# Work ahead of the first group in another order, the last group split 12 to 4: a convolution with a fused MLP

## The chip, the cores and the metric

The kernel runs on one core of a Trainium2 chip, in 32-bit floats throughout. The metric is the device time of one execution in microseconds (us). The core has a matrix engine (PE in the profile; its weight loads, which overlap, are listed as PEld), a vector engine (DVE), an activation engine (ACT), a general engine (POOL) and a queue engine (SP) that here only issues DMAs. Each engine takes its instructions in the order in which the program gives them; they meet through semaphores.

## The reference, cut to what matters

```python
# x: 8 x 4224 x 192, weight: 8 heads x 7 taps, g_ln: 192, w_ch1: 192 x 768, w_ch2: 768 x 192
w = softmax(weight, axis=-1)                       # 7 taps for each of 8 heads of 24 channels
y[b, s, h, :] = sum_k w[h, k] * x_pad[b, s + k, h, :]   # causal, 6 zero rows in front
mu, var = mean(y, -1), mean((y - mu)**2, -1)
xn  = (y - mu) / sqrt(var + 1e-6) * g_ln
out = y + max(xn @ w_ch1, 0) @ w_ch2
```

The inputs w_ch1 and w_ch2 are 64-bit floats in memory. The kernel reads them as pairs of 32-bit words and builds 32-bit floats from these itself.

## The kernel before, in words

**Groups.** The 33,792 tokens are worked on in 18 groups. A group has 128 partitions with n tokens each: group 0 has n = 6, group 1 n = 8, group 2 n = 10, and all from group 3 on n = 16. For each group the kernel convolves (`first_tap` and `second_tap` on ACT, `conv` on DVE, one instruction per tap and head), transposes 32 x 32 blocks on DVE (`transpose`), multiplies by w1 on PE (`up` for groups 0 to 2, `up_mixed` from group 3), evicts with a ReLU, multiplies by w2 (`down` for groups 0 and 1, `down_fast` from 2), transposes back and adds the result, scaled by the reciprocal root of the variance, to y. The scaling is put last because the ReLU lets a positive factor through. `up_mixed` and `down_fast` need seven products where a plain 2 x 2 block product needs eight; they form sums of quarters of their operands first (`sums_of_y`, `w1sums`, `w2sums`, `half_sum`).

**Order.** All orders are written out by hand (`manual_schedule`). PE runs `up(g)`, `down(g)`, `up(g+1)` and so on; the other engines prepare group g + 1 and finish group g - 1 meanwhile.

**Ahead of the first group** (lines 178 to 372 and 970 to 999). SP issues the load of w1's words in four pieces, then x of group 0 in three (`load_x`, L168 and L175). The taps go through a softmax. `split_words` (L232 to L245) takes mantissa and exponent out of each of three pieces of w1 (128 x 384 words each): DVE, ACT, DVE, DVE, ACT. `join_words` puts them together: L250 adds the low word (DVE), L253 sets the sign (DVE), L261 multiplies and applies g_ln, whose two columns `gs` ACT copies out of PSUM (L980). A memset of one word of `raw2` (L985) behind the first joined piece holds back the load of w2's words (L986) until then, and with it the eight loads of group 1's x that SP issues next (L142).

The convolution of group 0 is divided: DVE and ACT take heads 0 to 4, PE heads 5 to 7 (`PE_HEADS`). For a head on PE, ACT writes seven diagonal matrices, a tap each (`tap_matrices`, L319), PE multiplies x by them (`conv_on_pe`, L326), ACT copies the sum into y (L330). `centre_w1` subtracts the mean over the 192 channels from w1, so that mu drops out of the product: PE forms the means (L335, L339), ACT copies them (L342), and then PE makes four copies of each 32-row block of w1, in three steps of four (pieces s = 0, 2, 1), with the copy product L354 and the subtraction L359; ACT evicts them into `w1` (L364). The first step fills columns 0 to 383 of blocks 0 to 3, the second blocks 4 and 5, the third columns 384 to 767 of blocks 0 to 3. `up(0)` goes through six chunks f of 128 columns, so that chunks 0 to 2 read nothing of the third step. `keep_warm` (L369) issues idle matmuls of a constant tile `less`, which nobody reads.

The scratch tile `room` is cut into parts by `carve`, in the order of the calls. Group 0's hidden tile later lies on its first 4608 columns.

**During up(0).** ACT evicts each chunk (L525). The mantissa of w2 runs on DVE and ACT (`split_words`), its exponent is scaled by ACT behind chunk 0 (`scale_power`), and `join_words` makes w2 on DVE, all of it before the convolution of group 1. `first_tap(1)` takes heads 0 to 3 behind chunk 0 and 4 to 7 behind chunk 1. PSUM has eight banks: `take_bank` takes the next one, `take_set` the next aligned four, and each chunk of `up` takes four.

**The last group.** Its 16 tokens a partition are divided. `fast[NG - 1]` of them (11) go through `down_fast` with width 176; the hidden rows of the others are put aside by ACT (`keep`, L752), and `down_rows` (L959) multiplies six pieces of 128 for each such token. DVE adds each token to y (L942); one store takes all fast tokens (L949), and one each of the others.

Of the kernel before, what the change touches and what calls it, by code (L numbers as in the profile page):

```python
# [16 lines left out]
def kernel(  # L17
# [56 lines left out]


    fast = {g: groups[g][2] if g >= 3 else 0 for g in range(NG)}
    fast[NG - 1] = J - 5
    fast[2] = groups[2][2]
    NFAST = max(fast.values())
    T = C // 2  # L80
# [39 lines left out]
    def take_bank():  # L120
        i = turn[0] % 8
        turn[0] = i + 1
        return all_banks[:, i]
# [63 lines left out]
    def carve(n, dtype):  # L187
        part = room[:, taken[0] : taken[0] + n].bitcast(dtype)
        taken[0] += n
        return part  # L190

    less = carve(P, F32)
    nc.gpsimd.memset(less, -1.0 / C)

    raw1 = carve(6 * FH, U32).rearrange("p (s f w) -> p s f w", f=FH, w=2)
    raw2 = opool.tile([P, J * D], F32, tag="ot", name="raw2")[:, 0 : 2 * NF * D].bitcast(U32)
    raw2 = raw2.rearrange("p (n w) -> p n w", w=2)
    w1_words = moe_w_ch1.bitcast(U32)
# [45 lines left out]
    def scale_power(power):  # L244
        nc.scalar.activation(power, power, AF.Relu, scale=float(1 << 23), bias=low)  # L245

    def join_words(dst, raw, mant, power, g=None):
        lo, hi = raw[:, :, 0], raw[:, :, 1]
        mant, power = mant.bitcast(F32), power.bitcast(U32)
        nc.vector.scalar_tensor_tensor(  # L250
            out=mant, in0=lo, scalar=2.0**-52, in1=mant, op0=ALU.mult, op1=ALU.add
        )
        nc.vector.scalar_tensor_tensor(  # L253
            out=power, in0=hi, scalar=0x80000000, in1=power,
            op0=ALU.bitwise_and, op1=ALU.bitwise_or,
        )
        power = power.bitcast(F32)
        if g is None:
            nc.vector.tensor_tensor(dst, mant, power, op=ALU.mult)
            return  # L260
        nc.vector.scalar_tensor_tensor(  # L261
            out=dst, in0=mant, scalar=g, in1=power, op0=ALU.mult, op1=ALU.mult
        )
# [13 lines left out]
    nc.vector.tensor_tensor(  # L277
        taps, taps, wsum.unsqueeze(2).to_broadcast([P, H, K]), op=ALU.mult
    )
    words_1 = [(raw1[:, s], carve(FH, I32), carve(FH, I32)) for s in range(3)]  # L280

    w1 = consts.tile([P, NC, F], F32, name="w1")
    w2flat = consts.tile([P, NF * D], F32, name="w2")
    w2 = w2flat.rearrange("p (c d) -> p c d", d=D)
# [29 lines left out]
    def tap_matrices(h, ks=range(K)):  # L317
        for k in ks:
            nc.scalar.mul(diag[:, h - PE_HEADS[0], k, :], unit, taps[:, h, k : k + 1])  # L319
# [12 lines left out]
    def centre_w1():  # L332
        pm = [take_bank()[:, 0:FH] for r in range(2)]
        for r in range(2):
            nc.tensor.matmul(pm[r], share[0], w1f[:, r, :], start=True, stop=False)  # L335
            if r == 0:
                conv_on_pe(PE_HEADS[2])
        for r in range(2):
            nc.tensor.matmul(pm[r], share[1 + r], w1f[:, 2, :], start=False, stop=True)  # L339
        tap_matrices(PE_HEADS[1])  # L340
        for r in range(2):
            nc.scalar.copy(mean[:, FH * r : FH * r + FH], pm[r])  # L342
        conv_on_pe(PE_HEADS[0])
        conv_on_pe(PE_HEADS[1])

        for s, parts in (
            (0, [(q, 0) for q in range(NQ)]),
            (2, [(NQ, 0), (NQ + 1, 0), (NQ, 1), (NQ + 1, 1)]),
            (1, [(q, 1) for q in range(NQ)]),
        ):  # L350
            pw = [take_bank() for q in range(NQ)]
            for q in range(NQ):
                rows = slice(C * q, C * q + C)
                nc.tensor.matmul(  # L354
                    pw[q][:, 0:FH], copy[rows], w1f[rows, s, :], start=True, stop=False
                )
            for q, (c, r) in enumerate(parts):
                rows = slice(C * q, C * q + C)
                nc.tensor.matmul(  # L359
                    pw[q][:, 0:FH], less[rows], mean[rows, FH * r : FH * r + FH],  # L360
                    start=False, stop=True,
                )
            for q, (c, r) in enumerate(parts):
                nc.scalar.copy(w1[:, c, FH * r : FH * r + FH], pw[q][:, 0:FH])  # L364
    def keep_warm(times):

        idle = take_bank()
        for _ in range(times):
            nc.tensor.matmul(idle[:, 0:P], less, less, start=True, stop=True)  # L369

# [187 lines left out]
    def up(g):  # L558


        n = groups[g][2]
        hidden_tile(g)
        for f in range(NF):
            banks = take_set()
            rows_of_tiles(banks, yt[g][:, 0:n], w1[:, :, f * P : f * P + P])
            evict_up(g, f, banks[:, :, 0 : n * C])
            if g == 0 and f == 0:
                scale_power(words_2[2])
                join_words(w2flat, *words_2)
            if g == 0 and f < 2:  # L570
                first_tap(1, heads=(H // 2 * f, H // 2 * (f + 1)))
            between(g, f)

    def quarters_of_w1(f0=0, f1=FC):
# [392 lines left out]
            )  # L967


    keep_warm(17)  # L970
    g_cols = take_bank()
    for r in range(2):
        nc.tensor.matmul(
            g_cols[:, r : r + 1], g_row[:, P * r : P * r + P], ones[:, 0:1], start=True, stop=True
        )
    for s in range(3):
        split_words(*words_1[s])
        if s == 0:
            tap_matrices(PE_HEADS[2], range(3))
    nc.scalar.copy(gs, g_cols[:, 0:2])  # L980
    tap_matrices(PE_HEADS[2], range(3, K))
    for s in range(3):
        join_words(w1f[:, s], *words_1[s], ga if s < 2 else gb)
        if s == 0:
            nc.vector.memset(raw2[0:1, 0:1, :], 0)  # L985
    nc.sync.dma_start(  # L986
# [1 line left out]
        in_=w2_words.rearrange("(c p) d -> p c d", p=P),  # L988
    )
    load_x(1)  # L990
    first_tap(0, heads=(0, PE_HEADS[0]))
    tap_matrices(PE_HEADS[0])
    conv(0, heads=(0, PE_HEADS[0]))
    centre_w1()
    transpose(0)
# [16 lines left out]
    for g in range(NG):  # L1012
# [8 lines left out]
            work = []  # L1021
        if g == 0:
            early = CH * C // GRP
            conv(1, heads=(0, early))
            transpose(1, 0, CH)
            conv(1, heads=(early, H))
            first_tap(2)
            second_tap(2)
            let_in(w1sums[:, 1])
            transpose(1, CH, NC)  # L1030
            load_x(3)
            store_y(1)
            moments(0)
            moments(1)
            sums_of_quarters(w1sums[:, 1], w12, w22)
            sums_of_quarters(w1sums[:, 0], w11, w1sums[:, 1])
            next(root(0, True))
        elif g == 1:
            conv(2, 2)
            transpose(2)  # L1040
            first_tap(3)
            add_second_tap(3, 6)
            sums_of_quarters(w2sums[:, 2], b12, b22)
            sums_of_quarters(w2sums[:, 0], b12, b11)
            sums_of_quarters(w2sums[:, 1], b22, w2sums[:, 0])
            sums_of_quarters(w2sums[:, 3], b21, w2sums[:, 1])
            load_x(4, nc.gpsimd, pad=False)
            store_y(2, nc.gpsimd)
        elif g == 2:
            conv(3, 2, 5, heads=(0, 6))  # L1050
            lower_sum(2)
            conv(3, 5, K, heads=(0, 6))
            let_in(w1sums[:, 2])
            sums_of_quarters(w1sums[:, 2], w21, w1sums[:, 0])
# [54 lines left out]
```

## Time and profile before

| | |
|---|---|
| three timed runs | 956.90, 957.18, 958.33 us; median 957.18 |
| the profiled execution | 957.49 us, of which span 955.5 us |
| PE busy | 946.9 us (99%) |
| DVE / ACT / POOL busy | 891.3 / 699.0 / 337.1 us |
| granted PE clock | 1.00 |
| up(0) and down(0) on PE | 24.1 to 49.06 us |
| from the last group's first `down_rows` to the end of the span | 942.4 to 955.5 us |

A share of busy time is an average over the span. The span begins a little before the first instruction, and about 2 us of the execution lie outside it. In a timeline a line gives the start, the time from there to the end of the group, the engine, the line of the code, the operation, the tiles (written <- read), shapes and count; the bracket has the idle time before it and what ended it. A 32-bit matmul leaves two records in the trace, so that its counts are twice those of the program.

### The profile page before, as it was taken

How to read it: one execution, taken by the hardware profiler on the slowest of the kernel's cores; microseconds unless marked ns; L12 is line 12 of the kernel's file. 1: busy time of each engine (PE TensorE's matmuls, PEld its weight loads, DVE VectorE, ACT ScalarE, POOL GpSimd, SP SyncE). 2: the span in 40 equal slices, each digit the busy share in tenths (PEclk: the TensorE clock that was granted, in tenths of full speed). 3: DMA queues.
4: the chain of work that ended last, by engine and by line, in shares of the span. 5: the costliest groups of instructions: out<-in, count | busy, mean ns of one | idle time of the engine just before them, and what ended most of it. 6: DMA issues, size and time to landing. Idle time of an engine off the chain costs nothing.

```text
span 955.5 us, 38716 instructions
## 1 busy us (share of the span) xinstructions
PE 946.9 (99%) x17262; PEld 726.1 (76%) x17262; DVE 891.3 (93%) x1500; ACT 699.0 (73%) x1174; POOL 337.1 (35%) x472
## 2 busy tenths in 40 slices
PE   8999999999999999999999999999999999999998
PEld 6886896876869687786968778695867869586787
DVE  7999999999999999999999999999999999999757
ACT  6754678596877959687795968779695877967462
POOL 1157522623145141534227141452316332261320
PEclk9999999999999999999999999999999999999999
DMA  8359689689697988979697896969889696778251
GB/s 209 105 154 212 110 221 281 120 182 235 135 262 140 246 160 185 221 133 276 129 251 150 194 220 128 277 128 253 158 195 209 126 275 133 175 135 141 40 98 68
DMA packets 39691, 168.87 MB, mean 177 GB/s; under 512 B 4453, under 2 KB 8294, under 8 KB 33511
## 3 DMA queue, kind: packets, MB, share of 16 engines
q0 software_dynamic: 32576, 106.25, 60.0%
q1 hardware_dynamic: 6944, 60.16, 17.2%
q8 instruction: 135, 2.21, 0.9%
q14 instruction: 30, 0.25, 0.1%
q10 hardware_dynamic: 6, 0.00, 0.0%
HBM read 38.93 MB, written 50.33 MB: 93 GB/s over the span
## 4 chain that ended last, share of the span: by engine, by line
PE 95%; DMA 2%; ACT 1%; POOL 1%; issue 0%; SPq 0%; DVE 0%; ACTq 0%; POOLq 0%
PE ps L535 46%; PE ps L838 44%; PE ps L785 3%; PE ps L959 1%; DMA xg<-in_x_dram 1%; DMA room<-room 1%; PE ps L326 1%; ACT room L645 1%; ACT w L364 0%; POOL room L612 0%; POOL d L462 0%; POOL r L485 0%; POOL d L481 0%; ACT y L382 0%; ACT spare L245 0%
## 5 line engine op out<-in xcount | busy, mean ns | idle before, releaser
L419 DVE SCALAR_TENSOR_TENSOR y<-xg,taps,y 128x384 f32<-128x384 f32 (+3 forms) x720 | 362.6, 579 | 1.0 <-issue 0.8
L838 PE MATMUL ps<-room,w2sums 128*32 128x256 f32 (+2 forms) x4608 | 246.2, 370 | 0.4 <-issue 0.4
L535 PE MATMUL ps<-yt,w 32*128 32x256 f32 (+2 forms) x4104 | 235.5, 379 | 0.4 <-ACT room L525 0.4
L645 ACT COPY room<-ps 128x1024 f32<-128x1024 f32 (+1 forms) x135 | 175.0, 1296 | 78.4 <-PE ps L535 78.0
L535 PEld LDWEIGHTS ps<-yt,w 32*128 32x128 f32 x4104 | 204.6, 185 | 25.6 <-issue 9.0
L838 PEld LDWEIGHTS ps<-room,w2sums 128*32 128x32 f32 x4608 | 148.3, 110 | 92.4 <-ACT room L658 5.3
L838 PE MATMUL ps<-room,w 128*32 128x256 f32 (+2 forms) x3456 | 188.2, 370 | 0.1
L805 DVE TENSOR_TENSOR room<-room 128x1024 f32<-128x1024 f32 (+2 forms) x147 | 160.6, 1166 | 20.7 <-PE ps L838 20.7
L838 PEld LDWEIGHTS ps<-room,w 128*32 128x32 f32 x3456 | 111.3, 110 | 69.0 <-DVE room L651 5.0
L535 PE MATMUL ps<-ysums,w1sums 32*128 32x256 f32 x2160 | 125.6, 379 | 0.0
L535 PEld LDWEIGHTS ps<-ysums,w1sums 32*128 32x128 f32 x2160 | 109.4, 185 | 11.1 <-ACT room L645 3.6
L938 POOL DMA_DIRECT2D out_dram<-ot x69 | 59.3, 990 | 161.3 <-ACT ot L927 104.7
L411 POOL DMA_DIRECT2D y<-tb x59 | 52.5, 1386 | 152.7 <-ACT room L844 110.2
L844 ACT COPY cs<-ps 128x256 f32<-128x256 f32 (+2 forms) x192 | 69.9, 366 | 44.3 <-PE ps L838 44.3
L927 ACT ACTIVATE ot<-ot,r 128x192 f32<-128x192 f32 x232 | 93.8, 463 | 0.0
L658 ACT ACTIVATE room<-room 128x1024 f32<-128x1024 f32 (+1 forms) x89 | 92.8, 1072 | 1.4 <-DMA room<-parts_cs 1.2
L382 ACT ACTIVATE y<-xg,taps 128x384 f32<-128x384 f32 (+3 forms) x141 | 73.1, 611 | 1.5 <-DMA xg<-in_x_dram 1.5
L450 DVE BATCH_NORM_STATS2 st<-y 128x6 f32<-128x192 f32 x264 | 70.2, 345 | 0.0
L844 ACT COPY room<-ps 128x256 f32<-128x256 f32 (+2 forms) x96 | 35.2, 367 | 45.6 <-PE ps L838 43.6
L400 ACT ACTIVATE tb<-xg,taps 128x384 f32<-128x384 f32 (+1 forms) x120 | 65.9, 624 | 0.0
L535 PE MATMUL ps<-yt,w1sums 32*128 32x256 f32 x1080 | 65.3, 380 | 0.1
L535 PE MATMUL ps<-ysums,w 32*128 32x256 f32 x1080 | 64.5, 376 | 0.0
(113 smaller groups left out, 907.3 us busy)
## 6 DMA issues: line engine op xcount, KB each, us to landing
xg<-in_x_dram SPq DMA_DIRECT2D x14, 2112.0 KB, 16.5
room<-room POOLq DMA_DIRECT2D x45, 512.0 KB, 5.2
out_dram<-ot POOLq DMA_DIRECT2D x59, 384.0 KB, 9.4
y<-tb POOLq DMA_DIRECT2D x58, 384.0 KB, 8.8
out_dram<-y SPq DMA_DIRECT2D x13, 1536.0 KB, 9.1
room<-parts_cs POOLq DMA_DIRECT2D x28, 512.0 KB, 6.8
room<-parts_tb POOLq DMA_DIRECT2D x14, 1024.0 KB, 7.6
xg<-in_x_dram POOLq DMA_DIRECT2D x1, 2112.0 KB, 14.5
```

The costliest lines, as they stand in the source:

```text
L382: nc.scalar.mul(y[g][:, 0:n, cs], xg[g][:, 0:n, cs], taps[:, h, 0:1])
L400: nc.scalar.mul(tb[g][:, 0:n, cs], xg[g][:, 1 : 1 + n, cs], taps[:, h, 1:2])
L419: nc.vector.scalar_tensor_tensor(out=y[g][:, 0:n, cs], in0=t[:, k : k + n, cs], scalar=taps[:, h, k : k + 1], in1=y[g][:, 0:n, cs], op0=AL ...
L450: nc.vector.bn_stats(out=sums[g][:, j, :], in_=y[g][:, j, :])
L535: nc.tensor.matmul(banks[:, q, i * w : i * w + w], right[rows, c, P * i : P * i + P], left[rows, :, c, :], start=(first and c == 0 and i = ...
L645: nc.scalar.activation(dst, src, AF.Relu) if relu else nc.scalar.copy(dst, src)
L658: nc.scalar.activation(c, c, AF.Relu)
L805: nc.vector.tensor_tensor(a[:, *dst, f], a[:, *left, f], a[:, *right, f], op=op)
L838: nc.tensor.matmul(dst[C * q : C * q + C, 0:w], right[:, f, C * c : C * c + C], left[:, f, q], start=(first and f == PAIR), stop=(f == PAI ...
L844: nc.scalar.copy(to[:, c], dst[:, 0:w].rearrange("p (j t) -> p j t", t=t))
L927: nc.scalar.mul(ots[g][:, j, :], ots[g][:, j, :], rstd[g][:, j : j + 1])
L938: nc.gpsimd.dma_start(out=rows[:, d0:d1], in_=src[:, d0:d1], accum_op=ALU.add)
```

## The change

The last group's fast tokens go from 11 to 12, and the rest from five to four. The parts of `room` are cut in another order: w1's words and their work tiles first, which together are the 4608 columns of group 0's hidden tile, then `less` and the rest. `join_words` becomes three functions. On DVE the low word and sign of the first piece of w1 come ahead of the split of the third piece. On PE nine idle matmuls stand ahead of the columns of g_ln and fourteen behind them, and two more in `centre_w1` in place of the convolution of head 7, which moves behind the second mean product. On ACT `gs` is copied before the third split, four of head 5's matrices are made ahead of `first_tap(0)`, and the matrices of head 6 are made in two parts. The convolutions of heads 5 and 6 on PE are each followed by one step of copies of w1. The third step of copies moves behind chunk 1 of `up(0)`, with `scale_power` of w2 behind it. `first_tap(1)` takes heads 0 to 3 behind chunk 0, none behind chunk 1, two behind chunk 2 and two behind chunk 3. On DVE the convolution of group 1's first four heads is cut at tap 5, and the sign and product of w2 stand in the cut.

```diff
--- before.py
+++ after.py
@@ -74,7 +74,7 @@
 
 
     fast = {g: groups[g][2] if g >= 3 else 0 for g in range(NG)}
-    fast[NG - 1] = J - 5
+    fast[NG - 1] = J - 4
     fast[2] = groups[2][2]
     NFAST = max(fast.values())
     T = C // 2
@@ -189,10 +189,11 @@
         taken[0] += n
         return part
 
+    raw1 = carve(6 * FH, U32).rearrange("p (s f w) -> p s f w", f=FH, w=2)
+    words_1 = [(raw1[:, s], carve(FH, I32), carve(FH, I32)) for s in range(3)]
     less = carve(P, F32)
     nc.gpsimd.memset(less, -1.0 / C)
 
-    raw1 = carve(6 * FH, U32).rearrange("p (s f w) -> p s f w", f=FH, w=2)
     raw2 = opool.tile([P, J * D], F32, tag="ot", name="raw2")[:, 0 : 2 * NF * D].bitcast(U32)
     raw2 = raw2.rearrange("p (n w) -> p n w", w=2)
     w1_words = moe_w_ch1.bitcast(U32)
@@ -244,17 +245,21 @@
     def scale_power(power):
         nc.scalar.activation(power, power, AF.Relu, scale=float(1 << 23), bias=low)
 
-    def join_words(dst, raw, mant, power, g=None):
-        lo, hi = raw[:, :, 0], raw[:, :, 1]
-        mant, power = mant.bitcast(F32), power.bitcast(U32)
+    def join_low(raw, mant, power):
+        mant = mant.bitcast(F32)
         nc.vector.scalar_tensor_tensor(
-            out=mant, in0=lo, scalar=2.0**-52, in1=mant, op0=ALU.mult, op1=ALU.add
+            out=mant, in0=raw[:, :, 0], scalar=2.0**-52, in1=mant, op0=ALU.mult, op1=ALU.add
         )
+
+    def join_sign(raw, mant, power):
+        hi, power = raw[:, :, 1], power.bitcast(U32)
         nc.vector.scalar_tensor_tensor(
             out=power, in0=hi, scalar=0x80000000, in1=power,
             op0=ALU.bitwise_and, op1=ALU.bitwise_or,
         )
-        power = power.bitcast(F32)
+
+    def join_product(dst, raw, mant, power, g=None):
+        mant, power = mant.bitcast(F32), power.bitcast(F32)
         if g is None:
             nc.vector.tensor_tensor(dst, mant, power, op=ALU.mult)
             return
@@ -277,11 +282,6 @@
     nc.vector.tensor_tensor(
         taps, taps, wsum.unsqueeze(2).to_broadcast([P, H, K]), op=ALU.mult
     )
-    words_1 = [(raw1[:, s], carve(FH, I32), carve(FH, I32)) for s in range(3)]
-
-
-
-
     w1 = consts.tile([P, NC, F], F32, name="w1")
     w2flat = consts.tile([P, NF * D], F32, name="w2")
     w2 = w2flat.rearrange("p (c d) -> p c d", d=D)
@@ -334,37 +334,35 @@
         for r in range(2):
             nc.tensor.matmul(pm[r], share[0], w1f[:, r, :], start=True, stop=False)
             if r == 0:
-                conv_on_pe(PE_HEADS[2])
+                keep_warm(2)
+        conv_on_pe(PE_HEADS[2])
         for r in range(2):
             nc.tensor.matmul(pm[r], share[1 + r], w1f[:, 2, :], start=False, stop=True)
-        tap_matrices(PE_HEADS[1])
+        tap_matrices(PE_HEADS[1], range(3))
         for r in range(2):
             nc.scalar.copy(mean[:, FH * r : FH * r + FH], pm[r])
+        tap_matrices(PE_HEADS[1], range(3, K))
         conv_on_pe(PE_HEADS[0])
+        copies_of_w1(0, [(q, 0) for q in range(NQ)])
         conv_on_pe(PE_HEADS[1])
-
-        for s, parts in (
-            (0, [(q, 0) for q in range(NQ)]),
-            (2, [(NQ, 0), (NQ + 1, 0), (NQ, 1), (NQ + 1, 1)]),
-            (1, [(q, 1) for q in range(NQ)]),
-        ):
-            pw = [take_bank() for q in range(NQ)]
-            for q in range(NQ):
-                rows = slice(C * q, C * q + C)
-                nc.tensor.matmul(
-                    pw[q][:, 0:FH], copy[rows], w1f[rows, s, :], start=True, stop=False
-                )
-            for q, (c, r) in enumerate(parts):
-                rows = slice(C * q, C * q + C)
-                nc.tensor.matmul(
-                    pw[q][:, 0:FH], less[rows], mean[rows, FH * r : FH * r + FH],
-                    start=False, stop=True,
-                )
-            for q, (c, r) in enumerate(parts):
-                nc.scalar.copy(w1[:, c, FH * r : FH * r + FH], pw[q][:, 0:FH])
+        copies_of_w1(2, [(NQ, 0), (NQ + 1, 0), (NQ, 1), (NQ + 1, 1)])
+
+    def copies_of_w1(s, parts):
+        pw = [take_bank() for q in range(NQ)]
+        for q in range(NQ):
+            rows = slice(C * q, C * q + C)
+            nc.tensor.matmul(pw[q][:, 0:FH], copy[rows], w1f[rows, s, :], start=True, stop=False)
+        for q, (c, r) in enumerate(parts):
+            rows = slice(C * q, C * q + C)
+            nc.tensor.matmul(
+                pw[q][:, 0:FH], less[rows], mean[rows, FH * r : FH * r + FH],
+                start=False, stop=True,
+            )
+        for q, (c, r) in enumerate(parts):
+            nc.scalar.copy(w1[:, c, FH * r : FH * r + FH], pw[q][:, 0:FH])
+
     def keep_warm(times):
 
-        idle = take_bank()
         for _ in range(times):
             nc.tensor.matmul(idle[:, 0:P], less, less, start=True, stop=True)
 
@@ -565,10 +563,12 @@
             rows_of_tiles(banks, yt[g][:, 0:n], w1[:, :, f * P : f * P + P])
             evict_up(g, f, banks[:, :, 0 : n * C])
             if g == 0 and f == 0:
+                first_tap(1, heads=(0, H // 2))
+            elif g == 0 and f == 1:
+                copies_of_w1(1, [(q, 1) for q in range(NQ)])
                 scale_power(words_2[2])
-                join_words(w2flat, *words_2)
-            if g == 0 and f < 2:
-                first_tap(1, heads=(H // 2 * f, H // 2 * (f + 1)))
+            elif g == 0 and f < 4:
+                first_tap(1, heads=(2 * f, 2 * f + 2))
             between(g, f)
 
     def quarters_of_w1(f0=0, f1=FC):
@@ -967,20 +967,27 @@
             )
 
 
-    keep_warm(17)
+    idle = take_bank()
+    keep_warm(9)
     g_cols = take_bank()
     for r in range(2):
         nc.tensor.matmul(
             g_cols[:, r : r + 1], g_row[:, P * r : P * r + P], ones[:, 0:1], start=True, stop=True
         )
-    for s in range(3):
-        split_words(*words_1[s])
-        if s == 0:
-            tap_matrices(PE_HEADS[2], range(3))
+    keep_warm(14)
+    split_words(*words_1[0])
+    tap_matrices(PE_HEADS[2], range(3))
+    split_words(*words_1[1])
     nc.scalar.copy(gs, g_cols[:, 0:2])
+    join_low(*words_1[0])
+    join_sign(*words_1[0])
+    split_words(*words_1[2])
     tap_matrices(PE_HEADS[2], range(3, K))
     for s in range(3):
-        join_words(w1f[:, s], *words_1[s], ga if s < 2 else gb)
+        if s:
+            join_low(*words_1[s])
+            join_sign(*words_1[s])
+        join_product(w1f[:, s], *words_1[s], ga if s < 2 else gb)
         if s == 0:
             nc.vector.memset(raw2[0:1, 0:1, :], 0)
     nc.sync.dma_start(
@@ -988,8 +995,9 @@
         in_=w2_words.rearrange("(c p) d -> p c d", p=P),
     )
     load_x(1)
+    tap_matrices(PE_HEADS[0], range(4))
     first_tap(0, heads=(0, PE_HEADS[0]))
-    tap_matrices(PE_HEADS[0])
+    tap_matrices(PE_HEADS[0], range(4, K))
     conv(0, heads=(0, PE_HEADS[0]))
     centre_w1()
     transpose(0)
@@ -1021,7 +1029,11 @@
             work = []
         if g == 0:
             early = CH * C // GRP
-            conv(1, heads=(0, early))
+            join_low(*words_2)
+            conv(1, 1, 5, heads=(0, early))
+            join_sign(*words_2)
+            join_product(w2flat, *words_2)
+            conv(1, 5, K, heads=(0, early))
             transpose(1, 0, CH)
             conv(1, heads=(early, H))
             first_tap(2)
```

## The prediction

> **What bounds the kernel now.** I read the page first, then the chain of waits, then the timelines of the two ends. The page's first line says how much there is to win at all:
>
> ```profile
> PE 946.9 (99%) x17262; PEld 726.1 (76%) x17262; DVE 891.3 (93%) x1500; ACT 699.0 (73%) x1174; POOL 337.1 (35%) x472
> ```
>
> PE idles 8.6 us of the 955.5 us span. The chain says where. These are pieces of it in the first 55 us (start, duration, what):
>
> ```profile
> 3.51 8.84 DMA xg<-in_x_dram
> 12.44 1.95 PE ps L326 x14
> ...
> 24.61 1.35 ACT w L364 x3
> ...
> 28.85 1.37 ACT y L382 x4
> 30.22 0.71 ACT room L525
> 30.93 0.04 issue
> 30.97 6.25 PE ps L535 x144
> 37.23 11.84 PE ps L785 x288
> ```
>
> From 30.97 us on the chain is PE work, up and down products without a gap, until the last group; from there on an edit moves the end only through the two ends. The opening has 4.9 us of idle PE: 2.1 ahead of the first matmul, 1.75 before the first mean product, 0.7 until x is there (12.35 us), 0.37 before chunk 3 of up(0). In the middle of it two things run side by side toward up(0): PE's means and copies, and DVE's timeline:
>
> ```profile
> 8.02 0.36 DVE L232 TENSOR_SCALAR room<-room 128x384 uint32<-128x384 uint32 x1 [1.20 <-DMA room<-in_moe_w_ch_dram]
> ...
> 8.95 0.55 DVE L250 SCALAR_TENSOR_TENSOR room<-room 128x384 f32<-128x384 uint32 x1
> 9.42 0.55 DVE L253 SCALAR_TENSOR_TENSOR room<-room 128x384 uint32<-128x384 uint32 x1
> ...
> 13.81 8.46 DVE L419 SCALAR_TENSOR_TENSOR y<-xg,taps,y 128x144 f32<-128x144 f32 x30
> 22.38 1.38 DVE L430 STREAM_TRANSPOSE yt<-y 128x1152 f32<-128x1152 f32 x1
> ```
>
> DVE waits 1.20 us for the third piece of w1, with work at hand that needs only the first. The convolution starts at 13.81, behind the joins, though x came at 12.35. up(0) can't start before the transpose ends at 23.76; PE's copies end at 24.05, so that the two limits lie together.
>
> At the other end, DVE and PE:
>
> ```profile
> 931.52 7.31 DVE L805 TENSOR_TENSOR room<-room 128x704 f32<-128x704 f32 x9 [6.29 <-PE ps L838]
> ...
> 943.83 3.71 DVE L942 SCALAR_TENSOR_TENSOR y<-ot,r,y 128x192 f32<-128x192 f32 x11
> ...
> 952.42 0.42 DVE L942 SCALAR_TENSOR_TENSOR y<-ps,r,y 128x192 f32<-128x192 f32 x1 [1.53 <-PE ps L959]
> ```
> ```profile
> 942.37 10.02 PE L959 MATMUL ps<-w,kept 128*128 128x192 f32 x60
> ```
>
> DVE works without a gap from 931.52 to 948.2 and then waits for PE's rows; PE's last row decides, 952.40.
>
> **What the Trainium skill says.** "FP8 and Floating Point Precision", TensorE Precision Notes: true 32-bit matmuls take four passes. Sixteen columns more, four passes, four products side by side on a quarter of the array each, at the 2.4 GHz of the page below: 6.7 ns. The trace agrees: the down products of width 256 take 27.44/252 = 108.9 ns each, those of width 176 5.37/72 = 74.6 ns, so 6.9 ns for 16 columns. "TensorE: Matmul & The Clock Gate", Part 1: about 3.4 us of activity run at half the clock. The trace agrees: 4 records of idle matmuls in each half us from 3 to 5.5, 6 or 7 from 6.5 on. "DMA: Bandwidth & Descriptors", Anatomy of one DMA: some 2 us of a transfer are fixed, mostly the receipt for the last byte. The last store here lands 1.7 us after its issue. The same page, Queues, rings and completion order: an engine's ring is consumed in order, which matters for a small store behind a large one; the trace of before has no such pair close enough to show it.
>
> **The change, part by part.**
>
> *Opening, DVE.* The low word and sign of piece 0 (L250 and L253, 8.95 to 10.09 with their spacing, some 1.05 us) go into the 1.20 us wait. They need ACT's results of 5.32 and 6.19 us: there. The product needs `gs`, now third in ACT's order behind the second scaling (7.99): about 8.1, in time. So the joins end at 12.8 instead of 13.9. The convolution needs `first_tap(0)`, which starts when x lands, 12.37, and gives its first head at 12.78. ACT makes a head every 0.33 us and DVE takes one every 0.28, so the first five cost 0.2 us more: end 21.5, transpose to 22.9. That is 0.9 us earlier than 23.76.
>
> *Opening, PE.* 23 idle matmuls instead of 17 end near 9.5 (17 took 5.9 us; the six more at the fast pace of 0.17 to 0.24 us, plus g_ln's columns, 0.6). The first mean product waits for DVE's first piece at about 9.6: no cost; the two more, 0.4 us, lie before the second piece at 11.3. The matmuls after 12.4 ran at the fast pace before too (28 records of L326 in 3.43 us), so keeping warm gains nothing I can see. Then from 12.44: head 7 to 14.4, means to 15.7, head 5 to 17.4, copies of step 0 to 18.9 (their subtraction needs the means from ACT, 16.9), head 6 to 20.6, copies of step 2 to 22.1. ACT's eviction of head 6 is done at 21.0, before the transpose asks for it at 21.5. PE then idles 0.8 us for the transpose.
>
> *Third step of copies.* Before, it lay where PE was waiting for the transpose, and so was nearly free. Now it is eight matmuls between chunks 1 and 2, 1.35 us at the spacing of the timeline (two fours at 0.75 and 0.65), in PE's own time. up(0) is 6 chunks at 2.08 (144 records in 6.25): 12.5. So 22.95 + 12.5 + 1.35 = 36.8 without a stall; before, it ended at 37.2, since ACT's twelve evictions and w2's exponent (27.48 to 28.85) made chunk 3 wait 0.37 and the start lost as much. ACT's new order: evict chunk 0 at 25.2 to 25.95, first taps to 27.5, evict chunk 1 to 28.4, copies to 30.2, exponent to 31.4, evict chunk 2 to 32.3. Chunk 2 on PE wants chunk 1's banks at 28.45, chunk 3 the copies' banks at 30.6, chunk 4 chunk 2's at 32.7: each free by 0.05 to 0.4 us. Opening: **-0.35** us, between -0.9 (no startup loss) and +1.0 (one of these slacks missed).
>
> *w2 and group 1.* w2's product is done behind 16 convolution steps of 0.333: mantissa to 26.4, convolution to 32, sign and product to 34.7. down(0) asks at 36.8: hidden, 2 us of cover. DVE loses the waits of 1.19 and 0.47 us, so group 1's transpose ends near 47.3 against 49.4, before up(1) at 48.7. Nothing.
>
> *DMA queues.* The memset moves ahead 1.1 us, so SP issues w2's words at 9.7 and x of group 1 behind it: eight issues, the last one held by w2's landing (2.6 us). All shift by the same 1.1. POOL's order is unchanged. That w2 now starts before x of group 0 has landed is not shown before: between nothing (same ring, behind it) and +1 us; I take nothing. The cut of `room` costs nothing: no instruction more, and it frees group 0's evictions of `less` and the means.
>
> *The end, PE.* 252 down products 6.9 ns longer: +1.73 us. One token of `down_rows` less, 9.96/5 = 1.99: sum -0.26. ACT's twelve `keep` get shorter, in idle ACT.
>
> *The end, DVE and stores.* The third product ends 108 x 6.9 ns = 0.74 later. DVE then has nine half sums by 0.07 more, 0.31 in the other larger tiles, one add more at 0.34: +2.1, so twelve adds end at 949.65 instead of 947.5. The rows' adds catch up before the last, which ends at 952.58 instead of 952.84. But the large store, now 1.18 MB, is issued at 949.7, not 947.57. Before, 1.475 MB (eleven tokens and four rows) flowed from 948.15 to 952.2, at 360 GB/s, and the last row's store found the queue empty. Now twelve tokens and three rows are the same 1.475 MB, from 950.3 to 954.4; the last row's 98 KB are issued at 952.6 and follow behind, to 954.65, against 954.05 before. So the end comes **+0.5** later, between -0.26 (the queue drains faster, over 440 GB/s) and +0.9.
>
> **Sum.** -0.35 + 0.5 = +0.2, within its bounds nothing. Against the profiled 957.49 that is 957.7; that execution stood 0.3 above the median of three, so 957.4 as a median.
>
> **The rivals.**
> - *Both ends gain*: the starting losses of up(0) go (-0.6) and the last store isn't queued (-0.26): 956.3. For it: PE bounds everything between; against it: 360 GB/s measured in just that place. Still within 0.2%. More than 0.2% (1.9 us, about what a measurement of this kernel can tell from no change) would need two more idle stretches of PE to go, and x's landing at 12.35 and the convolution of 8.46 stand in the way.
> - *Group 1's x comes late: slower.* `first_tap(1)` now stands on ACT at 25.95 instead of 28.63, ahead of chunk 1's eviction, the copies, w2's exponent. If the last of the eight loads lands later than that, all of these wait, PE behind them, one to one. Before, its issue was at 17.46 and issue to landing took 7.8 to 9.2 us: 25.3 to 26.7, so only the 1.1 us shift keeps it clear. It passes 1.9 us from a landing at about 27.7; a landing at 28 gives 959.5. Against it: the bytes counted from 12.4 on are through by 23.5 even before.
> - *The idle matmuls matter*: if the clock had dropped at 12.4, PE's 9 us there would halve. The records exclude it; and DVE would bound it at the same place: 957.
>
> **Numbers.** Both ends nearly cancelling 0.68; both gain 0.14, half of it beyond 0.2% if an idle stretch goes that I hold for fixed; group 1's x or another missed slack 0.18, 0.13 of it beyond 0.2%. So faster 0.07, same 0.80, slower 0.13. The range of 955.7 to 959.2 adds both bounds of the two ends (-1.2 and +1.9) to 957.2, with 0.3 for the spread of the runs.
>
> **What would show it.** In the profile after: L250 and L253 inside the wait before 8 us; convolution from 12.8, transpose ending at 22.9; first up matmul at 23; L354 and L357 between 27 and 28.5 with PE busy; down(0) from 36.8 and up(1) at 48.7; twelve adds ending at 949.7, the last row at 952.1 on PE, and DMA traffic until 954.6 without the gap before the last store. A transpose still at 23.7, ACT waiting for x before `first_tap(1)`, or PE idle over 0.5 us within up(0) would make it wrong.

## The result, and the profile after

The changed kernel takes 964.88 us (median of four runs, 963.04 to 966.8) against 957.75 for the old one: 1.0075 times as long, 95% interval 1.0051 to 1.0099. It is **slower by about 7 us**. I had forecast 957.4 and no difference that can be measured; the range ended at 959.2. The profiled execution has a span of 963.9 us against 955.5, 8.4 longer.

The page's first line after, and its clock line (tenths of full speed in 40 slices):

```profile
PE 949.9 (99%) x17266; PEld 732.5 (76%) x17266; DVE 891.0 (92%) x1500; ACT 698.4 (72%) x1174; POOL 337.3 (35%) x472
...
PEclk9999899999999999999999999999999999999999
```

PE is 3.0 us busier with four records more. Eight more idle matmuls are under 2 us of that; the rest is work that ran slowly, and the clock line has its one digit below nine in the fifth slice (96 to 120 us). The chain of waits after, from the first up product to the fourth group, shows where PE loses its hold on it:

```profile
37.37 11.84 PE ps L785 x288
49.21 15.75 PE ps L533 x288
64.96 15.68 PE ps L785 x288
80.64 11.03 PE ps L533 x161
...
102.53 6.36 DVE y L417 x12
109.20 3.10 issue
112.29 1.32 DVE w L873
113.61 2.22 DVE room L805 x3
115.87 10.35 PE ps L838 x216
126.22 27.90 PE ps L533 x504
```

Up to 80.64 this is the old chain within 0.15 us. Then the activation and vector engines stand in it, in front of the down products of group 2. The old chain had PE alone in that place, with one gap of 0.43 us:

```profile
80.49 19.59 PE ps L535 x288
100.08 14.80 PE ps L838 x430
114.89 0.43 issue
115.32 2.88 PE ps L838 x73
118.19 1.92 PE ps L535 x29
```

From 126.22 on the chain after is the old one again, 8.03 us late. PE's timeline there:

```profile
115.87 7.90 PE L838 MATMUL ps<-room,w2sums 128*32 128x160 f32 x144 [5.65 <-DVE room L805]
123.60 2.62 PE L838 MATMUL ps<-room,w 128*32 128x160 f32 x72
126.15 2.22 PE L533 MATMUL ps<-yt,w 32*128 32x256 f32 x35
```

PE waits 5.65 us for DVE's half sums, and the 216 records behind the wait take 10.28 us where the old kernel needed 8.30, its gap of 0.43 counted in. Shares by stretch (us; busy and instructions of PE, PEld, DVE, ACT, POOL; granted clock; DMA share; GB/s) show the clock and the busy DVE:

```profile
105.00:112.00 7.00, 5.22 (x156) 4.89 (x146) 6.90 (x10) 3.62 (x10) 3.00 (x2) 1.00 0.02 5
112.00:118.00 6.00, 2.13 (x32) 1.58 (x36) 6.00 (x9) 0.23 (x1) 3.14 (x4) 0.73 0.89 159
118.00:124.00 6.00, 6.00 (x128) 4.80 (x124) 5.96 (x16) 1.38 (x6) 1.10 (x1) 0.70 0.71 133
```

DVE has hardly a gap here (6.90 of 7 us, then 6.00 of 6): it is late from before. Its timeline shows when it fell behind, and the last line what the old kernel did there (`L448` takes the statistics for the variance, called bn_stats below):

```profile
47.06 0.06 DVE L582 MEMSET w1sums<- 1x1 f32 x1
47.16 0.98 DVE L428 STREAM_TRANSPOSE yt<-y 128x768 f32<-128x768 f32 x1
48.06 3.69 DVE L448 BATCH_NORM_STATS2 st<-y 128x6 f32<-128x192 f32 x14
60.81 1.61 DVE L417 SCALAR_TENSOR_TENSOR y<-xg,taps,y 128x240 f32<-128x240 f32 x4 [9.06 <-DMA y<-tb]
```
```profile
53.19 8.91 DVE L419 SCALAR_TENSOR_TENSOR y<-xg,taps,y 128x240 f32<-128x240 f32 x22
```

It stands 9.06 us before the convolution of group 2. In the old kernel that began at 53.19, right behind the bn_stats. The wait is for `y<-tb`, the three transfers by which POOL adds group 2's second tap into y (`add_second_tap`). POOL issued them at 44.73, at 44.58 before. The tile's answer, after and then before:

```profile
L409 POOL DMA_DIRECT2D y<-tb x3: 1032/1208/1544, 44.7 to 46.0; - x3
...
DMA to landing us min/median/max: 4.2/12.9/14.6
```
```profile
L411 POOL DMA_DIRECT2D y<-tb x3: 1035/1211/1547, 44.6 to 45.9; - x3
...
DMA to landing us min/median/max: 4.1/5.6/7.1
```

Same issue, same 0.96 MB, the last of them 7.5 us later. What shares the DMA engines with them is group 3's x (2.1 MB) and then eight stores of group 1's y, both from SP. SP may issue that load once DVE has finished group 1's convolution, which gives its buffer back: at 48.50 before, at 47.20 after, since DVE is earlier by 1.3 us. After and then before:

```profile
47.20 0.33 SPq L151 DMA_DIRECT2D xg<-in_x_dram  x1
```
```profile
48.50 0.33 SPq L151 DMA_DIRECT2D xg<-in_x_dram  x1
```

The queues in one stretch of 2 us, 50 to 52 (packets over all 16 DMA engines, MB, share of the engines' time), after and then before:

```profile
q1 hardware_dynamic: 31, 0.52, 63.8%
q0 software_dynamic: 32, 0.10, 25.2%
```
```profile
q0 software_dynamic: 153, 0.24, 105.0%
```

Before, POOL's queue (q0) had the engines to itself until 52 and was done then; SP's queue (q1) moved nothing ahead of that, though the load had been issued at 48.50. After, the load's first packets came between 48.5 and 49. Between 49 and 50 it had ten packets and POOL's queue one. From 50 on the two had about equal counts: 31 and 32 in this stretch, 33 and 31 in the next, 34 and 37 in the one behind. A packet of the load is a row's 4224 floats, 17 KB; one of `y<-tb` 3 KB. So POOL's queue fell to 0.05 MB/us; in the old kernel it had 0.18 between 46 and 50. This is what the Trainium skill says in "DMA: Bandwidth & Descriptors", Queues, rings and completion order: an engine goes round the queue rows that have work, a packet at a time. The trace agrees with it from 50 us on, by these counts, if the profile's packets are the page's; the page's are bundles of descriptors, and no run here shows what such a bundle is. That the load of the old kernel got no turn from 48.5 to 52 the page doesn't explain ("POOL's transfers in one" returns to it). I had cited that very section for another sentence and passed over this one.

### The profile page after: what moved, and what is told of

It is laid out like the page before. It is cut to its first block, busy times and chain, and to the rows that moved or that the text cites. A ratio compares the mean times of both kernels' runs of the same rounds, so it can differ in the third digit from the quotient of the medians.

```text
span 963.9 us, 38718 instructions
## 1 busy us (share of the span) xinstructions
PE 949.9 (99%) x17266; PEld 732.5 (76%) x17266; DVE 891.0 (92%) x1500; ACT 698.4 (72%) x1174; POOL 337.3 (35%) x472
## 4 chain that ended last, share of the span: by engine, by line
PE 92%; DVE 3%; DMA 2%; POOL 1%; ACT 1%; issue 1%; SPq 0%; ACTq 0%; DVEq 0%; POOLq 0%
PE ps L533 46%; PE ps L838 43%; PE ps L785 3%; DVE y L417 2%; DMA xg<-in_x_dram 1%; PE ps L959 1%; DMA room<-room 1%; DVE room L805 0%; ACT room L645 0%; ACT room L523 0%; ACT y L380 0%; POOL room L612 0%; ACT ot L927 0%; POOL d L460 0%; POOL d L478 0%
## 5 line engine op out<-in xcount | busy, mean ns | idle before, releaser
L838 PE MATMUL ps<-room,w2sums 128*32 128x256 f32 (+2 forms) x4608 | 249.6, 374 | 5.7 <-DVE room L805 5.7
L838 PEld LDWEIGHTS ps<-room,w2sums 128*32 128x32 f32 x4608 | 155.0, 111 | 94.5 <-DVE room L805 6.0
L838 PEld LDWEIGHTS ps<-room,w 128*32 128x32 f32 x3456 | 114.3, 110 | 66.7 <-DVE room L651 5.0
L448 DVE BATCH_NORM_STATS2 st<-y 128x6 f32<-128x192 f32 x264 | 70.1, 349 | 0.0
```

The costliest lines, as they stand in the source:

```text
L448: nc.vector.bn_stats(out=sums[g][:, j, :], in_=y[g][:, j, :])
L838: nc.tensor.matmul(dst[C * q : C * q + C, 0:w], right[:, f, C * c : C * c + C], left[:, f, q], start=(first and f == PAIR), stop=(f == PAI ...
```

## The experiments

The theory from the two traces (theory 1 in the texts below): **DVE, earlier by 1.3 us, lets group 3's x start while `y<-tb` is still under way; `y<-tb` then lands 7.5 us late, DVE is late with all of group 2, PE waits for it, and the clock drops in the wait.** The rivals: the end with its 12 tokens; the new order or the cut of `room`; the small stores. Ratios stand for each run, since the old kernel, measured again beside them, had medians between 957.51 and 959.09.

**The end alone** (old kernel):

```diff
-    fast[NG - 1] = J - 5
+    fast[NG - 1] = J - 4
```

> The old kernel with the last group's split alone changed to 12 and 4. My prediction's step for the end: +0.5 us (PE -0.26, the queued store the rest), between -0.3 and +0.9, which is within 0.1% of the old kernel. Theory 1 (the loss is made near 53 us, by a transfer that comes too early): +0.3 to +0.5 us here, since the trace after shows 0.33 us more from the last group's first down product to the end. Rival (the split costs the time): +7 us.

Ratio 1.0004 (0.9994 to 1.0014). The split is not the cause. Whether it costs the 0.3 to 0.5 us expected, the interval doesn't tell.

**The load held back** (changed kernel): a memset of one word of the load's tile on DVE, behind six more DVE instructions (`gate=True` adds the memset). The stores of group 1's y stay behind the load.

```diff
-            load_x(3)
-            store_y(1)
             moments(0)
+            load_x(3, gate=True)
+            store_y(1)
             moments(1)
```

> The changed kernel, with the load of group 3's x held back behind the six bn_stats of group 0 on DVE (a memset of one word of its tile), so that SP issues it at about 49.7 us in place of 47.2. Theory 1 (that load, issued 1.3 us earlier than in the old kernel, overtakes the three accumulating transfers y<-tb of group 2, for which DVE then waits 9 us): they land by 54 us again, DVE's wait goes, PE has no wait behind the down products of group 2, and the time is 956.5 to 958.5 us. Rival (the new order of ACT and DVE, or the new cut of the scratch tile, makes group 2 late by itself): still 963 to 966.

957.56 us, ratio 0.9998 (0.9987 to 1.0008). The loss is gone; everything else of the change is in. SP issued the load at 49.4, POOL's first transfer went out at 44.4, and:

```profile
DMA to landing us min/median/max: 4.2/5.9/7.9
```

DVE's wait is 2.40 us, and PE has none for the half sums. The new orders and the new cut are cleared by this.

**The old kernel, with the load early.** Four convolution instructions are left out, so that DVE frees the buffer sooner. Group 1's output lacks a tap for four heads, and there are four DVE instructions fewer.

```diff
-            conv(1, heads=(early, H))
+            conv(1, 1, K - 1, heads=(early, H))
```

> The old kernel, whose convolution of group 1 leaves out the last tap of heads 4 to 7 (four DVE instructions of 0.33 us; group 1's result is then not the reference's), so that DVE frees group 1's x 1.3 us earlier and group 3's load is issued at about 47.2 us. Theory 1: the old kernel becomes slow in the same way, 963 to 966 us, with y<-tb landing 13 to 15 us after its issue. Rival (something else in the change makes group 2 late): 956 to 958.

965.37 us, ratio 1.0078 (1.0063 to 1.0092): less work, 7 us slower. The load went out at 46.8, 2.1 us behind POOL's first issue; `y<-tb` landed late, and PE stood before the half sums:

```profile
DMA to landing us min/median/max: 4.2/12.8/14.4
```
```profile
115.67 5.59 PE L838 MATMUL ps<-room,w2sums 128*32 128x160 f32 x88 [5.56 <-DVE room L805]
```

Together with the run before, this shows the cause: the time at which the load and the stores behind it go out switches the loss on and off, in both kernels. Which of the two it is, load or stores, these runs leave open; two runs below part them.

**Idle matmuls in the wait** (changed kernel), on PE in front of the fifth of the seven products:

```diff
+        if g == 2:
+            spot = all_banks[:, turn[0] % 8]
+            for _ in range(24):
+                nc.tensor.matmul(
+                    spot[:, 0:P], w2flat[:, 0:P], w2flat[:, 0:P], start=True, stop=True
+                )
         product(0, a[:, 1, 1], w2sums[:, 1], parts[0], False, 2)
```

> The changed kernel with 24 idle matmuls of 128 columns (0.22 us each, 5.3 us in all) on PE where it waits 5.65 us in the down products of group 2. After the wait the trace shows a granted clock of 0.50 for some 5 us, and 216 records took 10.35 us where the old kernel took 7.94. If that is the clock's answer to the wait, the time falls by 2.0 to 2.5 us, to about 962.5; if those products are slow for another reason (operands coming late, DMA), no change. The wait itself stays.

963.1 us, ratio 1.0059 (1.0046 to 1.0072), against 1.0075 for the changed kernel: 1.5 us less by the ratios, 1.8 by the medians, though the intervals overlap. The trace is clearer:

```profile
109.25 5.62 PE L885 MATMUL ps<-w 128*128 128x128 f32 x48
114.87 5.10 PE L838 MATMUL ps<-room,w2sums 128*32 128x160 f32 x144
```

The 144 records take 5.10 us, as in the old kernel, and not 7.90. Of these 2.8 us PE lost 0.91 again in a gap inside the last product. So some 2 us of the loss were the clock's answer to the wait, the rest the wait.

**How late is late enough.** The load held by one instruction (the transpose of 0.98 us), and by that and two bn_stats:

```diff
-            load_x(3)
+            load_x(3, gate=True)
```

> The changed kernel with the load of group 3's x held only behind the second transpose of group 1, one DVE instruction of 0.98 us, so that SP issues it some 3.4 us after POOL began to issue y<-tb (2.5 in the changed kernel: late; 3.9 in the old one and 5.0 with six bn_stats in front: in time). Theory 1 has a threshold between 2.5 and 3.9 and says nothing on where: in time, if two thirds of the 0.96 MB of y<-tb being through is enough (about 957.5 us), late if the last of the three transfers has to be nearly through (963 to 966). Rival (the place in SP's order, not the time, decides): as in the changed kernel, 964.

```diff
-            load_x(3)
-            store_y(1)
-            moments(0)
+            moments(0, 0, 2)
+            load_x(3, gate=True)
+            store_y(1)
+            moments(0, 2)
```

> The same with two bn_stats more in front, so that the load is issued some 3.9 us after POOL began to issue y<-tb, as in the old kernel. Theory 1: in time, about 957.5 us. Rival (the interval is not what counts): between 958 and 964.

Ratios 0.9999 (0.9990 to 1.0008) and 0.9996 (0.9986 to 1.0005). From POOL's first issue to SP's it was 3.5 and 4.0 us; the last transfer landed 8.1 and 7.1 us after its issue. So the whole loss comes between 3.5 us and 2.5 (changed kernel), counted from POOL's first issue. At 3.5 the last transfer is a little late and DVE waits 2.5 us instead of 9; PE doesn't feel it.

**Which transfer does it.** The stores late, the load early as in the changed kernel:

```diff
-            store_y(1)
...
             next(root(0, True))
+            store_y(1, nc.gpsimd)
```

> The changed kernel, where group 1's y is stored later (eight stores of 96 KB issued by POOL behind the root of group 0, near 58 us, in place of SP at 47.6), so that group 3's x, still issued at 47.2, is alone beside y<-tb. Theory 1 in its narrow form (that load alone is what y<-tb loses to: in the changed kernel each engine's queues took 31 and 32, 33 and 31, 34 and 37 packets in the same 2 us, but 17 KB a packet against 3): y<-tb still lands 12 to 14 us after its issue and the time is 962 to 966. Rival (the small stores behind it do the harm): y<-tb in time, 957 to 958.

963.9 us, ratio 1.0047 (1.0029 to 1.0064). `y<-tb` landed 4.2, 12.9 and 13.3 us after issue, PE waited 4.48: the load does most of it alone. What the stores add these runs don't fix: PE's wait was 1.17 us longer with them, and the ratio 1.0075 against 1.0047, with intervals that overlap. The opposite, stores early and load held:

```diff
-            load_x(3)
             store_y(1)
             moments(0)
+            load_x(3, gate=True)
             moments(1)
```

> The opposite: the stores issued by SP at 47.2, group 3's x held behind the six bn_stats as before and behind the stores. Theory 1, narrow: the stores' packets are of 6 KB, a third of the load's, and 0.79 MB in all, so y<-tb is some 2 to 4 us late instead of 7.5; DVE waits 4 to 6 us (2.4 with the load held and nothing early), and most of it is lost in the slack: 957.5 to 960. Rival (any early transfer does the whole harm): 963 to 966.

Ratio 1.0012 (1.0004 to 1.0021), 1.2 us. The last landing was 10.0 us, 2.9 over the old kernel, and DVE waited 4.46: smaller packets and fewer bytes, smaller harm. (SP, which had the stores in front, issued the load only at 55.3.)

**The load in small pieces**, as early as in the changed kernel:

```diff
-            queue.dma_start(
-                out=flat[:, 0 : (n + PAD) * D], in_=xr[b, :, (j0 - PAD) * D : (j0 + n) * D]
-            )
+            w, d0 = (n + PAD) * D, (j0 - PAD) * D
+            step = w // 8 if g == 3 else w
+            for d in range(0, w, step):
+                queue.dma_start(out=flat[:, d : d + step], in_=xr[b, :, d0 + d : d0 + d + step])
```

> The changed kernel, whose load of group 3's x is cut into eight loads of 528 columns, so that a row's piece is 2.1 KB in place of 17; issued from 47.2 on, some 0.35 us apart. If the engines take a turn per piece of a row (theory 1: equal counts of packets of unequal size), y<-tb (3 KB pieces) now gets more than half of the bytes and lands 8 to 10 us after its issue: DVE waits 2 to 5 us and the time is 957.5 to 960. If a turn holds several pieces, or the load's queue comes first whatever the size, nothing changes: 963 to 966.

Ratio 0.9996 (0.9986 to 1.0007): the loss is gone without holding anything back. The queues between 50 and 52:

```profile
q0 software_dynamic: 103, 0.24, 73.5%
q1 hardware_dynamic: 105, 0.20, 30.1%
```

Again equal counts, 103 and 105 (99 and 100 from 49 to 51.5, ahead of POOL's last and smaller packets), but now of 2.1 KB on the load's side. POOL's queue moves 0.24 MB here, against 0.10 in the changed kernel; from 49 to 51.5 it had 0.12 MB/us, still less than the 0.18 alone. The last landing was 9.2 us after issue, DVE waited 3.70, PE 0.39. So, once the two queues share the engines, the harm follows the size of the other's packets. (The eight issues also hold SP until 54.5, so that the stores come 7 us later; the run with the stores late had shown that this alone doesn't save the time.)

**POOL's transfers in one** (changed kernel). The threshold was too sharp for a matter of overlap. In every run that lost the 7 us, or most of them, the load's first packets came 1.6 to 2.0 us after SP began to issue it, within 0.6 us of where POOL's first transfer gave way to its second. In every run so far without the loss, with the load in one piece and ahead of the stores, they came only when POOL's queue had all but run dry, at 51 to 53, whatever the issue. Where the load was held behind six bn_stats, 5.0 us or more behind POOL's first issue, that took no longer than in the runs with the loss, 1.7 to 2.0 us. In the old kernel, with either end, and where the load was held by one or by three instructions it took 3.2 to 3.8.

```diff
-        step = 4 if upto == H else 8
+        step = n if g == 2 else 4 if upto == H else 8
```

> The changed kernel, whose y<-tb of group 2 is one transfer of 0.96 MB in place of two of 384 KB and one of 192. In the traces the load of group 3's x, once issued, either moves its first packet 1.3 to 1.5 us later, as POOL's first transfer gives way to the second near 48.3 us (changed kernel, and all slow ones), or nothing until POOL's queue has run dry at 51 to 52, though issued at 47.2 to 49.4 (old kernel, and all fast ones with that load in one piece). If it comes in only where one of POOL's transfers ends, there is no such place now: the load, issued at 47.2, starts near 52, y<-tb is in time by 54, 957 to 958.5 us. If the two queues take turns wherever they meet, y<-tb is as late as in the changed kernel or later: 963 to 967.

957.85 us, ratio 0.9992 (0.9981 to 1.0003): the loss is gone, though the load was issued at 46.5, 2.4 us behind POOL's issue at 44.1, as close as in the changed kernel. The queues in the half us from 50 to 50.5, and in that from 50.5 to 51:

```profile
q0 software_dynamic: 9, 0.07, 131.8%
...
q1 hardware_dynamic: 3, 0.05, 32.6%
q0 software_dynamic: 3, 0.00, 0.5%
```

The load waited some 4.3 us for its first packet, until `y<-tb` was through; that landed 7.9 us after its issue. This fits a load that takes turns with POOL's queue only if it gets in near the start of the second transfer. It doesn't prove that the change of transfer lets it in: one transfer also has packets of 7.7 KB in place of 3. And a change of transfer isn't enough: in the old kernel, and in the runs held by one and by three instructions, the load had been issued 1.7 to 2.2 us before POOL's second transfer gave way to the third (near 50.3, 49.5 and 50.0), and got nothing there. What lets the load in stays open.

**The opening by itself**, with the load held behind the six bn_stats as above and the old end:

```diff
-    fast[NG - 1] = J - 4
+    fast[NG - 1] = J - 5
```

Then the same with w2's words let in behind the second piece of w1:

```diff
-        if s == 0:
+        if s == 1:
             nc.vector.memset(raw2[0:1, 0:1, :], 0)
```

> The changed kernel's opening alone, with the load held behind six bn_stats and the last group at 11 and 5 again. My prediction's step for the opening: -0.35 us, so 957.1 where the old kernel stands at 957.5; against the run with the split (957.56) -0.3, if the end costs 0.3. Rival (the opening gains nothing, since x of group 0 lands later by what DVE's joins gain): as the old kernel, or up to 0.3 slower.

> As the run before it, with the memset that lets in w2's words moved behind the second joined piece of w1, so that SP issues them at about 11.1 us, as late as the old kernel did, in place of 9.5. In the changed kernel's profile x of group 0 landed 9.46 us after its issue, in the old one 8.84. If w2's words get in the way of that x: it lands near 12.35 again, and the time is 0.3 to 0.6 us below the run before it. If the landing only varies from run to run (8.5 to 9.5 in the profiles so far): no difference.

Ratios 0.9996 (0.9986 to 1.0007) and 0.9996 (0.9987 to 1.0005). My -0.35 us for the opening fits, and so does nothing. Group 0's x landed 9.4 and 9.1 us after its issue in these two; over all profiles it was 8.5 to 9.7 with w2's words early, 8.4 to 9.1 with them late. So w2's words are not shown to get in its way, and the landing varies by more than the change of order can win. No version beats the old kernel by more than can be measured; the one with POOL's transfers in one comes nearest, at 0.9992.

## Why the prediction was wrong

**The step that failed** is the one on w2 and group 1: DVE's transpose of group 1 "ends near 47.3 against 49.4, before up(1) at 48.7. Nothing." The size was nearly right (48.1), the price was not. I asked who waits for the transpose, and nobody does. I did not ask what else DVE's earlier end releases. The old kernel's SP queue has a 2.1 MB load at 48.50; my paragraph on DMA queues followed the loads up to 18 us and stopped there. By the timelines, the convolution's earlier end shifts that load by 1.3 us, to where two of the three transfers of `y<-tb` are still to come. In place of "Nothing" the runs showed the last of these landing 14.6 us after its issue instead of 7.1, and PE 5.65 us idle. With the load, and the stores behind it, held back, the loss was gone (0.9998), and with the stores alone late it was not (1.0047).

**The frame that let it pass** was "from there on an edit moves the end only through the two ends". The reading under it was wrong too: the old chain does leave PE, though PE stays busy, for activation engine, general engine and a DMA between 731.25 and 751.2, and PE itself has the gap of 0.43 us at 114.89 shown above. And a busy PE doesn't mean slack elsewhere: in the old kernel, DVE came to the half sums of group 2 only 0.40 us before PE released them.

```profile
107.42 6.71 DVE L805 TENSOR_TENSOR room<-room 128x640 f32<-128x640 f32 x9 [0.40 <-PE ps L838]
```

It was that close to being the limit 50 us on, so a delay of 7.6 us at 53 could reach PE nearly whole (6.05 us later at its next product).

**Step by step.** *Opening, DVE:* joins by 12.8, measured 12.7; right. x landed at 12.98 instead of 12.35, so that the convolution began at 13.51; I had priced that at nothing with up to +1 us, and it was within. Transpose end 22.9, measured 23.92: beside x's landing, DVE was idle for 0.52 us ahead of the transpose, which I had not foreseen. That stretch is there, 0.51 us or longer, in every run with the new opening and in none with the old one; what DVE waits for in it the profile doesn't settle. *Opening, PE:* right in mechanism: it idled 1.03 us for the transpose (0.8 forecast), copies between chunks 1 and 2 without a stall, up(1) at 49.14 or 0.15 after the old time by the chain, where I had -0.35; the late transpose took more than that. *The idle matmuls* ended at 10.2. My own terms sum to 10.2 to 10.6 (from 2.67: 5.9, 0.6 and six at 0.17 to 0.24), not to the 9.5 that I wrote; so the first mean product began at 10.01, 0.5 us after its operand was there. It cost nothing, because PE then stood 1.00 us for x. Whether these matmuls gain anything no run shows apart. The slow start of the old kernel's idle matmuls, which I read from the counts of records, shows in these alone: the granted clock reads 1.00 in the same stretch, 3 to 8 us. *w2's cover:* product at 35.6, down(0) at 37.3; hidden, as said. *The end:* PE's last row came 0.4 us sooner relative to the first down product, and a row's store landed 2.2 us after issue where the old ones took 1.6 to 1.8; from the first down product to the end it is 32.7 us against 32.35, +0.33 for the +0.5 forecast. The mechanism holds in the trace. (The page that I took a transfer's fixed 2 us from states it for DMAs that the general engine issues; these stores are SP's, and 1.6 to 2.2 is what they took.)

**The rivals.** I did have one that ended slower by a transfer that comes late, but on the wrong buffer: group 1's x, waited for by `first_tap(1)`. That one was in time; ACT went through it at 27.05 without a wait. I gave slower 0.13 in all. (The upper end of the range is 959.4 by its own terms, not 959.2; 964.88 is beyond both.) The sum of what was measured: +0.15 from the opening, 5.9 more until PE's delayed product starts, 1.98 behind it (the slow clock, less the 0.43 that PE stood there in the old kernel), +0.33 at the end, 8.4 us.

## What to carry to other kernels

An engine that finishes sooner gives back buffers sooner, and a load that waits for them starts sooner; list what every shifted engine releases, on every queue, until the next barrier, and see what those transfers will meet. Where a small accumulating transfer that somebody waits for can meet a large load that nobody needs yet, hold the load by a word's memset, cut its rows into pieces, or make the accumulation one transfer: each took back all of the 7 us here. And when PE is 99% busy, look at how late the others were before calling them hidden.

## What the runs showed of the hardware

- Two queues that were both moving on the same DMA engines had equal counts of packets, not of bytes: 31 and 32 in 2 us, and 103 and 105 with pieces of 2.1 KB. A queue with 3 KB packets fell to 0.05 MB/us beside one with 17 KB packets, from 0.18 alone.
- A load issued 2.1 to 2.5 us behind the first of another queue's three transfers got its first packet 1.6 to 2.0 us after its issue and held the others up; issued 3.5 to 4.0 us behind, it got none for 3.2 to 3.8 us, until that queue was all but empty. So a shift of its issue by 1 us moved the time by 7. With the three transfers made one, a load issued 2.4 us behind waited some 4.3.
- A wait of 5.65 us on PE was followed by some 5 us at a granted clock of 0.50, which cost 2 us more; idle matmuls in the wait kept the clock (5.10 us for the 144 records, not 7.90).
